# The gate's x made behind the last weight split, and the first pair group's weights prepared one unit earlier

## The chip, the cores and the metric

The kernel runs on one core of a Trainium2 chip. The metric is the time of the device in microseconds (us), lower is better. The kernel before was timed three times: 843.56, 845.28 and 845.81 us, median 845.28 us. Its profiled execution took 846.12 us.

## The reference

Three layers follow one another, all in float32.

```python
# attention: B, H, S, D = 2, 8, 768, 64; a band of 96 local keys and 8 global ones
scores = q @ k.T / sqrt(D) - slope[h] * dist ; masked outside the band
x = softmax(scores) @ v                       # -> x: 1536 tokens x 512
# experts: 4 of them, 512 -> 1024 -> 512, weighted by given probabilities p
for e in range(4):
    out += p[:, e:e+1] * (relu(x @ w1[e]) @ w2[e])
# gate
a = out @ w1 ; b = out @ w2                   # 512 -> 1024
result = (a * b) @ w3 @ w_out                 # 1024 -> 1024 -> 512
```

## The kernel before, in words

Every large matrix product is made with three TensorE matmuls: an operand is split into a high part (a rounding cast) and a low part (what the cast lost), and high x high, low x high and high x low are summed in PSUM. `split` (line 47) does this: ScalarE writes the high part (line 49) and VectorE or GpSimd the low part (line 50). `three` (line 53) issues the three matmuls (lines 55, 56, 57). One matmul is 128x128 by 128x512.

Tokens are cut into three chunks c of 512; `x_hi[c]`, `x_lo[c]` hold the split x of a chunk, `acc[c]` the sum over experts. Weights lie in eight slots (`slots[0]` to `slots[7]`), each a high and a low tile of 128x1024: an expert's up weights in columns 0 to 511, its down weights in columns 512 to 1023. Raw weights come by DMA into tiles `wr`, of which the pool has two, so a load can only start when the split of the load before the previous one has read its tile.

The stages after attention:

- Units. `work` lists units (e, c, f): expert, chunk, block of 128 of the hidden 1024. Unit n issues the up product, a ReLU with its split (lines 541 and 542), and the down product of the unit two back. Experts 0 and 1 take all chunks here, experts 2 and 3 chunk 0 only.
- Pair groups. For experts 3 and 2, chunks 1 and 2 are done together by a scheme with seven products in place of eight (`Pairs`). A group's weights need the splits of raw blocks (`split_w`) and of sums of blocks (`sums_of_w`). Those of group n+1 are made inside group n. Those of group 0 are made in the last units, behind the ReLU of unit len-2 (`split_w`) and of unit len-1 (`sums_of_w`).
- The end of the pair groups ("the join" below). The last down products of expert 2 are issued, chunk 1 (f = 6, 7), then chunk 2 in the order f = 7, 4, 0, 1, 2, 3, 5, 6. As a slot becomes free, it takes weights for the next stage: slots 4, 0, 1, 2, 3, 5, 6, 7 are split in that order from eight raw loads (w3 transposed in slots 4 to 7, w_out in slots 0 to 3). When a chunk's down products are done, VectorE multiplies the four PSUM results by p into temporaries `t` (line 749) and GpSimd adds them to `acc` (line 750). For expert 2, `last_x(c, d)` then makes the split of the finished x: ScalarE casts (line 756), GpSimd subtracts (line 757). It is called for chunks 1 and 2 right behind their addition, and for chunk 0 after the last split.
- w34. TensorE makes w3 @ w_out, eight products of 24 matmuls into four PSUM banks `z`, each of them split into `w34h`, `w34l`. Chunk 2's down results stand in the same four banks, so the first product of w34 needs the first of them read by line 749.
- Gate: chunk 0 first, then chunks 1 and 2 as a pair, with w34 as the last product. It is the first reader of the x of `last_x`.

The order on every engine is the order in which the code issues, since the kernel sets its own schedule and each engine takes its queue in order. SP issues all the DMAs, in order as well.

Of the kernel before, what the change touches and what calls it, by code (L numbers as in the profile page):

```python
# [26 lines left out]
KC, FC = DM // P, F // P  # L27
CW = 512
NCH = N // CW
# [23 lines left out]
def three(nc, out, wh, wl, xh, xl, start, stop):  # L53

    nc.tensor.matmul(out, wh, xh, start=start, stop=False)  # L55
    nc.tensor.matmul(out, wh, xl, start=False, stop=False)  # L56
    nc.tensor.matmul(out, wl, xh, start=False, stop=stop)  # L57
# [24 lines left out]
def expert_shares(nc, g, tmp, room):  # L82

    nt = N // P
    pr = room[:nt, 0 : E * P].rearrange("c (t e) -> c t e", e=E)
    pe = room[:nt, E * P :].rearrange("c (e t) -> c e t", e=E)
    sm = tmp()[:nt, 0:P]
    nc.vector.tensor_reduce(sm, pr, axis=AX.X, op=ALU.add)
    nc.vector.tensor_scalar(sm, sm, 1e-9, None, op0=ALU.add)
    nc.vector.reciprocal(sm, sm)  # L90
    nc.vector.tensor_tensor(
        pe, pr.rearrange("c t e -> c e t"), sm.unsqueeze(1).to_broadcast([nt, E, P]), op=ALU.mult
    )
    nc.sync.dma_start(g.prob_dram.rearrange("e (c t) -> c e t", t=P), pe)


def banded_flag(nc, g, pool, ps, room):


    top, row, ok = room[:, 0:1], room[0:1, 8:16], room[0:1, 16:24]  # L100
    tp = ps.tile([P, CW], F32, name="z")[0:1, 0:P]
    nc.tensor.transpose(tp, top, g.ident)
    nc.vector.tensor_reduce(row[:, 0:1], tp, axis=AX.X, op=ALU.max)
    w0 = g.words[0:1]
    nc.vector.tensor_scalar(ok[:, 0:1], row[:, 0:1], 5.0e8, None, op0=ALU.is_le)
    nc.vector.tensor_scalar(ok[:, 1:2], w0[:, 0:1], 0.0, None, op0=ALU.is_ge)
    nc.vector.tensor_scalar(ok[:, 2:3], w0[:, 0:1], float(GW), None, op0=ALU.is_le)
    nc.vector.tensor_scalar(ok[:, 3:4], w0[:, 1:2], 0.0, None, op0=ALU.is_equal)
    nc.vector.tensor_scalar(ok[:, 4:5], w0[:, 2:3], 1.0, None, op0=ALU.is_ge)
    nc.vector.tensor_scalar(ok[:, 5:6], w0[:, 2:3], float(LW + 1), None, op0=ALU.is_le)  # L110
    nc.vector.tensor_scalar(ok[:, 6:7], w0[:, 3:4], 0.0, None, op0=ALU.is_equal)
    nc.vector.memset(ok[:, 7:8], 1.0)
    nc.vector.tensor_reduce(row[:, 1:2], ok, axis=AX.X, op=ALU.min)
    nc.vector.tensor_copy(g.flag, row[:, 1:2])
# [454 lines left out]
def pair_weights(g, pairs):  # L569

    half = lambda e, gr, c: g.w_moe[e, 2 * gr : 2 * gr + 2][:, :, c * CW : (c + 1) * CW].rearrange("f p c -> p f c")
    groups = [(e, gr) for e in pairs for gr in range(FC // 2)]
    res = [half(*groups[0], 0)]
    for n, (e, gr) in enumerate(groups):
        if n + 1 < len(groups):
            res.append(half(*groups[n + 1], 0))
        if e != pairs[0]:
            res.append(half(e, gr, 1))
    return res + [g.w3t_f32[0]] + [g.wo_f32[j] for j in range(4)] + [g.w3t_f32[j] for j in range(1, 4)]
# [105 lines left out]
def experts_and_gate(tc, g, x_hi, x_lo, slots, experts, first_time):  # L685
# [3 lines left out]
    with ExitStack() as ctx:  # L689
# [18 lines left out]
        def load_slot(s, src):  # L708

            raw = pool.tile([P, F], F32, name="wr")  # L710
            nc.sync.dma_start(raw, src)
            coming.append((s, raw))

        def land(keep=0):
            while len(coming) > keep:
                s, raw = coming.pop(0)
                split(nc, *slots[s], raw)

        work, pending = experts.work, experts.pending
        pieces = list(g.pieces) if first_time else []  # L720

        pairs = list(range(E - 1, EARLY - 1, -1))
# [3 lines left out]
        def down(e, c, f, fs=None, tail=False):  # L726
            fs = fs or list(range(FC))
            hi, lo = slots[f]
            hh, hl = pending.pop((e, c, f))
            if f == fs[0]:  # L730
                state["o"] = [
                    ps_z.tile([P, CW], F32, name="z") if tail else ps_a.tile([P, CW], F32, name=f"o{d}")
                    for d in range(KC)
                ]
            if f == fs[3]:
                state["p"] = xp.tile([P, CW], F32, name="prob")
                nc.sync.dma_start(state["p"], g.prob_dram[e, c * CW : (c + 1) * CW].partition_broadcast(P))
            o = state["o"]
            for d in range(KC):
                ds_ = slice(CW + d * P, CW + (d + 1) * P)  # L740
                three(nc, o[d], hi[:, ds_], lo[:, ds_], hh, hl, f == fs[0], f == fs[-1])
            ring.give((e, c, f))
            if f == fs[-1]:
                for d in range(KC):
                    if e == 0:
                        nc.vector.tensor_tensor(acc[c][:, d], o[d], state["p"], op=ALU.mult)
                        continue
                    t = tmp()
                    nc.vector.tensor_tensor(t, o[d], state["p"], op=ALU.mult)  # L749
                    nc.gpsimd.tensor_tensor(acc[c][:, d], acc[c][:, d], t, op=ALU.add)  # L750
                    if c and e == pairs[-1]:
                        last_x(c, d)

        def last_x(c, d):

            nc.scalar.copy(x_hi[c][:, d], acc[c][:, d])
            nc.gpsimd.tensor_tensor(x_lo[c][:, d], acc[c][:, d], x_hi[c][:, d].bitcast(F32), op=ALU.subtract)  # L757
# [15 lines left out]
        by_pairs = raws = xsums = None  # L773
        first_pair = len(work) - 2 * FC
        for n, w in enumerate(work):
            if n >= done:
                experts.up(w, ps_z.tile([P, CW], F32, name="z"))
                if n >= FC:
                    land()
                elif coming:  # L780
                    s = coming[-1][0] + 1
                    land(len(coming) - 1)
                    if s < FC:
                        load_slot(s, g.w_moe[0, s])
            if n == 4 and first_time:
                expert_shares(nc, g, tmp, room)
            if n == FC and first_time:
                flag_room = tmp()
                nc.vector.tensor_reduce(flag_room[:, 0:1], g.negmax, axis=AX.X, op=ALU.max)
            if n == FC + 2 and first_time:  # L790
                banded_flag(nc, g, pool, ps_z, flag_room)
            if n >= LAG:
                e, c, f = work[n - LAG]
                down(e, c, f)

                if e + 1 < E and (e >= EARLY or c == NCH - 1):
                    load_slot(f, g.w_moe[e + 1, f])
            if n > 4 and n % FC != LAG - 1:
                if ended:
                    nc.sync.dma_start(*ended.pop(0))  # L800
                if begun:
                    piece, dst = begun.pop(0)
                    ended.append((dst, convert_end(nc, cpool, *piece)))
                if fetched:
                    raw, dst = fetched.pop(0)
                    begun.append((convert_start(nc, cpool, raw), dst))
                if pieces:
                    src, dst = pieces.pop(0)
                    raw = cpool.tile([P, 512], mybir.dt.int64, name="raw", bufs=3)
                    nc.sync.dma_start(raw, src)  # L810
                    fetched.append((raw, dst))
            if by_pairs is None and n >= first_pair and not (pieces or fetched or begun or ended):
                late.close()
                tpool = of_experts.enter_context(tc.tile_pool(name=name + "xt", bufs=1))
                by_pairs = Pairs(nc, tpool, tmp, ps_z, experts)
                xsums = by_pairs.sums_of_x()
            elif xsums:
                next(xsums, None)
            if n == len(work) - 4:
                assert not coming  # L820
                raws = Raws(nc, pool, 2, pair_weights(g, pairs))
            if n == len(work) - 2:
                by_pairs.split_w(0, raws.here[0])
            if n == len(work) - 1:
                by_pairs.sums_of_w(0, raws.here[0])
                raws.used()
        assert next(xsums, None) is None
# [6 lines left out]
        for n in range(last + 1):  # L834
            i, gr = divmod(n, FC // 2)
            e = pairs[i]
# [43 lines left out]
        split(nc, *slots[7], raws.here[0])  # L880
        raws.used()
        assert not raws.here
        for d in range(KC):
            last_x(0, d)
        ring.free.remove((xp, "h3"))
        of_experts.close()

# [247 lines left out]
def tile_attention_experts_gate(  # L1135
# [43 lines left out]
    slots += slot_tiles(rest, 4, FC)  # L1179

    experts_and_gate(tc, g, x_hi, x_lo, slots, experts, True)

    banded = nc.values_load(g.flag[0:1, 0:1], min_val=0, max_val=1)
# [69 lines left out]
```

## Time and profile before

| | before |
|---|---|
| runs, median | 845.28 us (843.56 to 845.81) |
| profiled execution, its time | 846.12 us |
| its span (first to last instruction) | 844.3 us |
| TensorE matmul busy | 825.6 us, 98% |
| VectorE / ScalarE / GpSimd busy | 515.8 / 289.1 / 308.6 us |
| mean granted TensorE clock | 0.991 |

The 1.8 us between the profiled time and the span lie outside the instructions. A share of busy time is a mean over all stages, so the places where TensorE is not busy have to be found in time: of the page's 40 slices, the one from 591 to 612 us has a busy share of 6 tenths and a granted clock of 7 tenths, where the others after attention have 9 in both. It holds the end of the pair groups and the beginning of w34.

### The profile page before, as it was taken

How to read it: one execution, taken by the hardware profiler on the slowest of the kernel's cores; microseconds unless marked ns; L12 is line 12 of the kernel's file. 1: busy time of each engine (PE TensorE's matmuls, PEld its weight loads, DVE VectorE, ACT ScalarE, POOL GpSimd, SP SyncE). 2: the span in 40 equal slices, each digit the busy share in tenths (PEclk: the TensorE clock that was granted, in tenths of full speed). 3: DMA queues.
4: the chain of work that ended last, by engine and by line, in shares of the span. 5: the costliest groups of instructions: out<-in, count | busy, mean ns of one | idle time of the engine just before them, and what ended most of it. 6: DMA issues, size and time to landing. Idle time of an engine off the chain costs nothing.

```text
span 844.3 us, 11129 instructions
## 1 busy us (share of the span) xinstructions
PE 825.6 (98%) x4006; PEld 670.5 (79%) x4006; DVE 515.8 (61%) x962; ACT 289.1 (34%) x609; POOL 308.6 (37%) x318
## 2 busy tenths in 40 slices
PE   8999999999999999999999999999699999999996
PEld 4777888888888888888888888888488888888875
DVE  7998355557755557778557664673343733887840
ACT  6997321223321213333324321332242332333210
POOL 3687013535356554642154252314250002433300
PEclk9999999999999999999999999999799999999998
DMA  7762243557453458643101111121433220201011
GB/s 221 224 196 75 77 122 104 163 166 241 156 163 112 158 153 235 217 147 100 38 25 52 38 46 42 50 71 35 145 101 99 75 75 26 99 26 51 1 54 51
DMA packets 38710, 89.23 MB, mean 106 GB/s; under 512 B 3896, under 2 KB 10344, under 8 KB 38644
## 3 DMA queue, kind: packets, MB, share of 16 engines
q1 hardware_dynamic: 38644, 88.41, 33.5%
q8 instruction: 34, 0.56, 0.3%
q14 instruction: 32, 0.26, 0.1%
HBM read 74.74 MB, written 13.66 MB: 105 GB/s over the span
## 4 chain that ended last, share of the span: by engine, by line
PE 40%; issue 7%; POOL 2%; DVE 2%; ACT 1%; DMA 1%; ACTq 0%; POOLq 0%; DVEq 0%
PE z L55 9%; PE z L57 9%; PE z L56 9%; PE o L57 4%; PE o L55 4%; PE o L56 4%; POOL acc L750 1%; DMA wr<-wo_d 1%; ACT sh L49 1%; POOL sl L50 1%; DVE sl L50 1%; POOL xl L757 0%; DVE t L649 0%; DMA wr<-w3t_d 0%; DVE t L642 0%
## 5 line engine op out<-in xcount | busy, mean ns | idle before, releaser
L57 PE MATMUL z<-xh,sl 128*128 128x512 f32 x428 | 166.6, 389 | 0.0
L55 PE MATMUL z<-xh,sh 128*128 128x512 f32 x428 | 166.5, 389 | 0.0
L56 PE MATMUL z<-xl,sh 128*128 128x512 f32 x428 | 166.5, 389 | 0.0
L50 POOL TENSOR_TENSOR sl<-wr,sh 128x256 fp32r<-128x256 f32 (+1 forms) x44 | 40.9, 945 | 155.8 <-ACT sh L49 155.5
L498 POOL TENSOR_TENSOR cr<-cr,cb 128x512 f32<-128x512 f32 x40 | 51.6, 1290 | 125.2 <-issue 118.7
L57 PEld LDWEIGHTS z<-xh,sl 128*128 128x128 f32 x428 | 80.3, 188 | 17.1 <-DVE sl L50 0.2
L56 PEld LDWEIGHTS z<-xl,sh 128*128 128x128 f32 x428 | 80.3, 188 | 16.7
L55 PEld LDWEIGHTS z<-xh,sh 128*128 128x128 f32 x428 | 80.3, 188 | 16.6
L50 DVE TENSOR_TENSOR sl<-wr,sh 128x1024 fp32r<-128x1024 f32 (+1 forms) x57 | 67.8, 1198 | 41.8 <-ACT sh L49 41.1
L49 ACT CAST sh<-wr 128x1024 fp32r<-128x1024 f32 (+2 forms) x101 | 75.2, 767 | 11.9 <-DMA wr<-wo_d 8.1
L750 POOL TENSOR_TENSOR acc<-acc,t 128x512 f32<-128x512 f32 x36 | 47.5, 1350 | 84.1 <-DVE t L749 84.1
L483 POOL TENSOR_SCALAR ca<-ca 128x512 f32<-128x512 f32 x40 | 61.5, 1538 | 36.9 <-DMA raw<-in_w_out_dram 36.9
L55 PE MATMUL z<-sh,sh 128*128 128x512 f32 x128 | 51.1, 400 | 7.8 <-DVE t L749 7.8
L649 DVE TENSOR_TENSOR t<-t,z 128x512 f32<-128x512 f32 x56 | 37.5, 680 | 30.4 <-PE z L57 30.2
L57 PE MATMUL z<-sh,sl 128*128 128x512 f32 x128 | 50.9, 397 | 0.0
L56 PE MATMUL z<-sl,sh 128*128 128x512 f32 x128 | 50.8, 397 | 0.0
L269 ACT ACTIVATE pt<-t,negmax 128x256 f32<-128x256 f32 (+1 forms) x96 | 45.9, 480 | 9.0 <-DVE negmax L262 7.7
L308 POOL TENSOR_TENSOR pt<-pt,r 128x256 f32<-128x256 f32 (+1 forms) x72 | 40.8, 595 | 15.2 <-DVE r L237 12.6
L262 DVE CUSTOM_DVE_ANT_0 t<-sp,bias 128x256 f32<-128x256 f32 (+1 forms) x96 | 34.6, 394 | 1.8 <-ACT bias L224 0.4
L55 PEld LDWEIGHTS z<-sh,sh 128*128 128x128 f32 x128 | 24.7, 193 | 13.4 <-issue 8.2
L50 POOL TENSOR_TENSOR sl<-t,sh 128x256 fp32r<-128x256 f32 (+1 forms) x24 | 23.0, 972 | 31.2 <-ACT sh L49 31.0
L55 PE MATMUL o<-h0h,sh 128*128 128x512 f32 x84 | 32.8, 390 | 0.0
(254 smaller groups left out, 1751.9 us busy)
## 6 DMA issues: line engine op xcount, KB each, us to landing
wr<-in_w_moe_dram SPq DMA_DIRECT2D x44, 512.0 KB, 4.3
raw<-in_w3t_dram SPq DMA_DIRECT2D x16, 512.0 KB, 4.3
raw<-in_w_ab_dram SPq DMA_DIRECT2D x16, 512.0 KB, 4.6
wr<-wab_d SPq DMA_DIRECT2D x16, 512.0 KB, 3.3
raw<-in_w_out_dram SPq DMA_DIRECT2D x8, 512.0 KB, 5.1
w3t_d<-cr SPq DMA_DIRECT2D x16, 256.0 KB, 2.4
wab_d<-cr SPq DMA_DIRECT2D x16, 256.0 KB, 2.5
wr<-w3t_d SPq DMA_DIRECT2D x8, 512.0 KB, 3.4
```

Source lines behind the costliest of these rows:

```text
L49: nc.scalar.copy(hi, src)
L50: (lo_engine or nc.vector).tensor_tensor(lo, src, hi.bitcast(F32), op=ALU.subtract)
L55: nc.tensor.matmul(out, wh, xh, start=start, stop=False)
L56: nc.tensor.matmul(out, wh, xl, start=False, stop=False)
L57: nc.tensor.matmul(out, wl, xh, start=False, stop=stop)
L262: nc.vector.tensor_tensor_reduce(out=t[:, 0:w], in0=sp[hh % 2][:, hh // 2, 0:w], in1=bb, scale=-SCALE, scalar=3.0e38, op0=ALU.add, op1=ALU ...
L269: nc.scalar.activation(pt[:, hh, 0:w], t[:, 0:w], AF.Exp, bias=g.negmax[:, u * H + h : u * H + h + 1], scale=-1.0, accum_out=sums[:, h : h ...
L308: nc.gpsimd.tensor_tensor(pt[:, hh, 0:w], pt[:, hh, 0:w], r[:, hh : hh + 1].to_broadcast([P, w]), op=ALU.mult)
L483: nc.gpsimd.tensor_scalar(a, a, 2.0**-15, None, op0=ALU.max)
L498: nc.gpsimd.tensor_tensor(rest, rest, top.bitcast(F32), op=ALU.add)
L649: add = lambda o, a, b: nc.vector.tensor_tensor(o, a, b, op=ALU.add)
L750: nc.gpsimd.tensor_tensor(acc[c][:, d], acc[c][:, d], t, op=ALU.add)
```

## The change

Two edits. In the first, `last_x` is no longer called behind the additions of chunks 1 and 2; all twelve calls (three chunks of four) stand behind the split of slot 7. In the second, `split_w` and `sums_of_w` of the first pair group are issued one unit earlier, behind units len-3 and len-2; the load of the next raw tile, which `raws.used()` issues, moves with the sums.

```diff
@@ down
                     nc.gpsimd.tensor_tensor(acc[c][:, d], acc[c][:, d], t, op=ALU.add)
-                    if c and e == pairs[-1]:
-                        last_x(c, d)
@@ units
             if n == len(work) - 4:
                 assert not coming
                 raws = Raws(nc, pool, 2, pair_weights(g, pairs))
+            if n == len(work) - 3:
+                by_pairs.split_w(0, raws.here[0])
             if n == len(work) - 2:
-                by_pairs.split_w(0, raws.here[0])
-            if n == len(work) - 1:
                 by_pairs.sums_of_w(0, raws.here[0])
                 raws.used()
@@ after the last split
-        for d in range(KC):
-            last_x(0, d)
+        for c in range(NCH):
+            for d in range(KC):
+                last_x(c, d)
```

The first place is ScalarE's queue at the join. In the names, sh_1556, sh_1558, sh_1560, sh_1562 are the high tiles of slots 4, 5, 6, 7; sh_77, sh_79, sh_81, sh_83 those of slots 0 to 3; xh_71, xh_72, xh_73 the high x of chunks 0, 1, 2. Before:

```order
L756 CAST xh_72<-acc_1577 128x512 x4
L49 CAST sh_1556<-wr 128x1024
L49 CAST sh_77<-wr 128x1024
L49 CAST sh_79<-wr 128x1024
L49 CAST sh_81<-wr 128x1024
L49 CAST sh_83<-wr 128x1024
L49 CAST sh_1558<-wr 128x1024
L756 CAST xh_73<-acc_1578 128x512 x4
L49 CAST sh_1560<-wr 128x1024
L49 CAST sh_1562<-wr 128x1024
L756 CAST xh_71<-acc_1576 128x512 x4
```

And now:

```order
L49 CAST sh_1556<-wr 128x1024
L49 CAST sh_77<-wr 128x1024
L49 CAST sh_79<-wr 128x1024
L49 CAST sh_81<-wr 128x1024
L49 CAST sh_83<-wr 128x1024
L49 CAST sh_1558<-wr 128x1024
L49 CAST sh_1560<-wr 128x1024
L49 CAST sh_1562<-wr 128x1024
L754 CAST xh_71<-acc_1576 128x512 x4
L754 CAST xh_72<-acc_1577 128x512 x4
L754 CAST xh_73<-acc_1578 128x512 x4
L49 CAST w34h<-z 128x512 x2
```

The four casts of chunk 1 no longer stand ahead of slot 4's split, nor those of chunk 2 between slots 5 and 6. On GpSimd the twelve subtractions (line 757, now 755) follow the eight additions in one run, where they stood one behind each addition. VectorE's order at the join is unchanged.

The second place is ScalarE's queue in the last units, where the names h0 to h3 are the hidden tiles of the units and sh_77 to sh_83 slots 0 to 3. The difference:

```order
 L541 ACTIVATE h1h<-z 128x512
-L541 ACTIVATE h2h<-z 128x512
-L49 CAST sh_77<-wr 128x512
-L49 CAST sh_79<-wr 128x256
-L541 ACTIVATE h3h<-z 128x512
+L49 CAST sh_77<-wr 128x512
+L49 CAST sh_79<-wr 128x256
+L541 ACTIVATE h2h<-z 128x512
 L49 CAST sh_79<-t 128x256
 L49 CAST sh_81<-t 128x512
 L49 CAST sh_83<-t 128x256
+L541 ACTIVATE h3h<-z 128x512
```

The casts of the raw blocks now stand ahead of the ReLU of the last but one unit, and those of the sums ahead of the last unit's. On VectorE the four instructions that make the sums (line 642) move ahead of the low part of h3 in the same way.

## Rows read from the trace of the kernel before

**Rows 1.** Page, part 1: busy us, share of the span, instructions.

```profile
PE 825.6 (98%) x4006; PEld 670.5 (79%) x4006; DVE 515.8 (61%) x962; ACT 289.1 (34%) x609; POOL 308.6 (37%) x318
```

**Rows 2.** Waits of TensorE: line, for whom; us in total, times, longest.

```profile
PE z L55 <- DVE t L749: 7.8, 1, 7.8
...
PE z L57 <- POOL sl L50: 0.2, 1, 0.2
```

**Rows 3.** Timeline of TensorE, join: start, us, what, [idle before <-releaser].

```profile
583.45 0.39 PE L57 MATMUL z<-xh,sl 128*128 128x512 f32 x1
...
594.56 0.39 PE L55 MATMUL z<-h0h,sh 128*128 128x512 f32 x1
...
597.05 0.39 PE L57 MATMUL z<-h0h,sl 128*128 128x512 f32 x1
605.24 0.76 PE L55 MATMUL z<-sh,sh 128*128 128x512 f32 x1 [7.80 <-DVE t L749]
...
611.19 0.40 PE L57 MATMUL z<-sh,sl 128*128 128x512 f32 x1
```

**Rows 4.** Windows: stretch, us, busy PE, PEld, DVE, ACT, POOL, PEclk, DMA, GB/s.

```profile
600.00:601.00 1.00, 0.00 (x0) 0.00 (x0) 0.64 (x1) 0.00 (x0) 0.00 (x0) 0.88 0.83 262
601.00:602.00 1.00, 0.00 (x0) 0.00 (x0) 0.00 (x0) 0.00 (x0) 0.00 (x0) 0.50 0.90 246
```

**Rows 5.** Timeline of ScalarE at the join.

```profile
575.78 0.62 ACT L756 CAST xh<-acc 128x512 fp32r<-128x512 f32 x1 [3.46 <-POOL acc L750]
...
585.61 0.62 ACT L756 CAST xh<-acc 128x512 fp32r<-128x512 f32 x1 [2.65 <-POOL acc L750]
586.13 2.00 ACT L49 CAST sh<-wr 128x1024 fp32r<-128x1024 f32 x2
...
596.44 1.05 ACT L49 CAST sh<-wr 128x1024 fp32r<-128x1024 f32 x1 [3.21 <-DMA wr<-wo_d]
...
602.19 1.04 ACT L49 CAST sh<-wr 128x1024 fp32r<-128x1024 f32 x1 [2.80 <-DMA wr<-w3t_d]
```

**Rows 6.** Timeline of VectorE at the join.

```profile
604.41 2.48 DVE L749 TENSOR_TENSOR t<-z,prob 128x512 f32<-128x512 f32 x4
```

**Rows 7.** Timeline of SP's DMA issues at the join.

```profile
568.22 21.94 SPq L561 DMA_DIRECT2D wr<-wo_d  x3
...
588.71 1.45 SPq L561 DMA_DIRECT2D wr<-wo_d  x2
590.21 0.42 SPq L737 DMA_DIRECT2D prob<-prob_d  x1
...
598.77 0.32 SPq L561 DMA_DIRECT2D wr<-w3t_d  x1
```

**Rows 8.** Raw loads, line 561: landing times in 555 to 557, and 566 to 610.

```profile
DMA to landing us min/median/max: 3.3/3.3/3.3
...
DMA to landing us min/median/max: 3.2/3.4/6.5
```

**Rows 9.** Timeline of GpSimd at the join.

```profile
605.17 1.27 POOL L750 TENSOR_TENSOR acc<-acc,t 128x512 f32<-128x512 f32 x1 [17.57 <-DVE t L749]
...
619.37 7.01 POOL L757 TENSOR_TENSOR xl<-acc,xh 128x512 fp32r<-128x512 f32 x4 [1.12 <-ACT xh L756]
```

**Rows 10.** Timeline of TensorE at the first pair group.

```profile
429.21 0.39 PE L56 MATMUL z<-t2l,sh 128*128 128x512 f32 x1
429.77 0.50 PE L57 MATMUL z<-t2h,sl 128*128 128x512 f32 x1 [0.17 <-POOL sl L50]
430.11 0.40 PE L55 MATMUL z<-t2h,sh 128*128 128x512 f32 x1
```

**Rows 11.** Timelines there: GpSimd, ScalarE, SP.

```profile
427.34 3.07 POOL L50 TENSOR_TENSOR sl<-t,sh 128x256 fp32r<-128x256 f32 x3 [4.45 <-ACT sh L49]
...
419.73 0.60 ACT L541 ACTIVATE h2h<-z 128x512 fp32r<-128x512 f32 x1 [4.84 <-PE z L57]
...
395.77 10.89 SPq L561 DMA_DIRECT2D wr<-in_w_moe_dram  x2
```

## The prediction

> **What bounds the kernel now.** The page's first part comes first: TensorE is busy for 98% of the span [rows 1]. A faster TensorE is not on offer, so what can be won is the time in which it stands or runs at its lower clock. The second view is the list of TensorE's waits: one entry is far above the others, 7.8 us, once, for VectorE's line 749 [rows 2]. The third is TensorE's timeline at that place [rows 3]. The last down matmul starts at 597.05, the first matmul of w34 at 605.24. In the group of twelve before, starts lie (597.05 - 594.56) / 11 = 0.226 us apart, so 8.19 - 0.23 = 7.96 us are lost. Then the clock: from 605.24 to 611.19 fourteen matmuls start, which at 0.226 would take 3.17 us and took 5.95, so 2.78 us more are lost. The windows say why [rows 4]: the granted clock, still 1.00 before, is 0.88 in 600 to 601 and 0.50 after, so it fell to its lower level at about 600.76, in the middle of the standstill. The join costs 10.7 us in all.
>
> Why VectorE was late is read backwards. Line 749 for chunk 2 starts at 604.41 [rows 6], though the first of the four sums it reads was complete soon after 594.56 + 3 x 0.23 = 595.24. It stands in VectorE's queue behind the low part of slot 5. That waited for ScalarE's cast of slot 5 at 602.19, and that for a load (w3t_d) [rows 5]. The load was issued at 598.77 [rows 7], right when the split of slot 2 had read its tile, and slot 2's cast at 596.44 again waited for a load, issued at 588.71 + 1.45 - 0.32 = 589.84, when slot 0's split had read its tile. So it is a chain with two tiles: cast, low part, load, cast. Its beginning is at 586.13: ScalarE cast slots 4 and 0 there, back to back, since up to 585.61 it was taken up by the four casts of chunk 1's x, each behind a GpSimd addition (575.78 the first, 585.61 the last) [rows 5]. TensorE had released slot 0 long before: the group of f = 0 ends with the matmul at 583.45, thus at 583.84 [rows 3], and slot 4's group ended 2.72 us (12 x 0.226) earlier, at 581.12.
>
> **The change, edit 1: the join.** The chain now starts when TensorE lets it. Two steps recur in it. From a cast's start to the issue of the load that reuses its tile: 598.77 - 596.44 = 2.33 us [rows 5, 7] (cast, low part, SP). From slot 5's cast to TensorE's restart: 605.24 - 602.19 = 3.05 us (cast, low part, line 749, bank released) [rows 3, 5]. Now slot 4 is cast at 581.15 and slot 0 at 583.90; its load went out at 568.22 [rows 7] and is there. The load that slot 2 needs is issued at 583.90 + 2.33 = 586.23. It lands after D2, and slot 2's cast starts. 2.33 later the load for slot 5 is issued, and lands after D1; 3.05 after that TensorE restarts:
>
> 586.23 + D2 + 2.33 + D1 + 3.05 = 591.61 + D1 + D2.
>
> For the landing times the trace gives 3.3 for a load alone with a p load behind it, and 3.2 to 6.5, median 3.4, at the join [rows 8]. The 6.5 is the very load of slot 2 (589.84 to 596.44, 6.60 with ScalarE's start): it went out 1.1 us behind another raw load and 0.4 us ahead of a p load [rows 7]. The p load stays behind it, and the raw load before it is now issued 2.7 us earlier, not 1.1. I take D2 = 4.2, nearer to the lone load, bounds 3.3 and 6.6. D1 was 602.19 - 598.77 = 3.42; now a load for slot 3 may still be under way, so I take 3.6, bounds 3.3 and 3.8. The restart is then 591.61 + 7.8 = 599.4, with bounds 598.2 and 602.0; it could not be before about 597.8, since slot 5's own group of down matmuls ends only at 594.56 + 0.16 and the 3.05 follow. Gain of the wait: 605.24 - 599.4 = 5.84 us.
>
> With a restart at 599.4 TensorE has stood for some 2.1 us. In the trace the clock was at its upper level until 600.76 [rows 4], later than that, so I count all of the 2.78 us as won.
>
> The Trainium skill has a rule on this (TensorE: Matmul & The Clock Gate, Part 1: The HAM clock gate): the clock halves only after TensorE has been idle for a stretch, and comes back after a stretch of sustained work, whose position against the kernel's work varies from run to run. The trace agrees with both halves of it, once each. By that rule a restart at 599.4 keeps the clock for certain, and one after 600.8 may keep or lose it, whereas by the row alone it loses it.
>
> **What the moved work may cost.** The twelve x casts (0.62 us each [rows 5], 7.4 us at most) now stand on ScalarE between slot 7's split and the cast of w34's first product, which is queued behind them. The last four wait for GpSimd's additions, which begin behind line 749, at about 599.3, and take 1.3 each [rows 9], so they end near 605.3 and the first w34 cast comes at some 606. TensorE ends that product at 599.4 + 24 x 0.226 + 0.16 = 605.0, and wants its bank back for the fifth product, 4 x 24 x 0.226 = 21.7 us after the restart, at 621. That leaves 14 us of cover: cost 0, and 1 us for each beyond it. The next slots' splits are queued behind as well, but belong to products after the fourth. GpSimd's twelve subtractions run on from 605.3 at 1.75 each (7.01 for four [rows 9]) to 626. The gate, their first reader, begins behind eight products of 5.4 us, at about 643, and reads chunk 0 first, which is done first. Cost 0. VectorE's low parts of slots 6 and 7 follow line 749 at about 601.2; TensorE needs slot 6 at 599.4 + 2 x 5.43 = 610.3. Cost 0 as well. As for a gain from these, none: nothing waits for x earlier.
>
> **Edit 2: the first pair group.** TensorE waits once for the low part of the sums: 429.77 - 429.21 = 0.56 in place of 0.23, and 430.11 - 429.77 = 0.34 in place of 0.23 [rows 10], so 0.44 us. GpSimd made these low parts at 427.34 to 430.41 [rows 11]. One unit (24 x 0.226 = 5.4 us) earlier they end at 425.0, and nothing of TensorE's comes so late: gain 0.44, and no more, because no other wait stands there. What is now ahead of the ReLU h2h at 419.73 are two casts, in a gap of 4.84 us in which ScalarE waited for TensorE [rows 11]; the raw tile they read was asked for at 395.77, 19 us before. Cost 0, at worst that of a load that lands late, which even 6.6 us would not make it. The load behind `raws.used()` goes out earlier, and with it no queue is held up: SP issues it in order and has nothing ahead of it.
>
> **Sum.** 5.84 + 2.78 + 0.44 = 9.06 us. The profiled execution goes from 846.12 to 837.1. It lies 0.84 above the median of the runs, 845.28; from the median the same gain gives 836.2, my prediction.
>
> **Rivals.**
>
> 1. The loads stay slow, and the clock falls. D2 = 6.6, D1 = 3.8: restart at 602.0, behind 600.76, and the fourteen slow matmuls remain. Gain 3.2 + 0.44 = 3.7: 841.6. For it: the 6.5 us landing stood next to this p load. Against: less is under way beside it now.
> 2. The clock falls in the short standstill too. Gain 5.84 + 0.44 = 6.3: 839.0. Against it are the rows of the windows, for it only that the fall may come at another point of the standstill in another run.
> 3. The change doesn't do what it says: line 749 is late for a reason other than the x casts, for instance as the tiles of `wr` turn over no faster than before. Then only edit 2 is left: 844.8, no change. For it: line 749 waited for a chain of loads, with ScalarE idle for 3.21 and 2.80 us between casts [rows 5]. Against: the chain is tied to its beginning, and that moves, slot 4's cast from 586.13 to 581.15 and the load for slot 2 from 589.84 to 586.23.
> 4. Slower. The loads are bunched at the join: slots 4, 0, 1 are released at TensorE's pace of 2.72 us, so the raw loads of slots 1, 2 and 3 and the p load queue up at the DMA engines while down matmuls run. TensorE restarts later than before when D1 + D2 exceeds 605.24 - 591.61 = 13.6; at 8.3 each the restart is at 608.2, 3.0 us later, with the clock down: 847.8. Against: two tiles allow no more than two raw loads at a time, and with two and p under way the longest took 6.6.
>
> **How the numbers follow.** The forecast has 0.70, with its own range 834.6 (restart at 597.8: 7.44 + 2.78 + 0.44 = 10.7) to 838.5; rival 1 has 0.14, rival 2 0.07, rival 3 0.06, rival 4 0.03. A range from 834.0 to 841.7 holds the forecast, rival 2 and about the middle of rival 1. A measurement of this kernel can tell about 0.3%, 2.5 us, from no change. Faster than 842.7: 0.70 + 0.14 + 0.07 = 0.91; same: 0.06; slower: 0.03.
>
> **What would show it.** Right: in the changed kernel's ScalarE timeline slot 4's cast follows TensorE's release within a few tenths, about 5 us earlier than before; line 749 for chunk 2 starts near 598.6; TensorE's wait for it is about 2 us; the granted clock stays at 1.00 through the join; the wait for GpSimd's low parts at the first pair group is gone, and no new entry of over 0.5 us stands in the list of waits. Wrong: a restart after 602, a landing of over 6 us on the load of slot 2, a wait of w34's fifth product for a bank, or a wait of the gate for GpSimd.

## The result and the profile after

The changed kernel takes 835.19 us (median of 4 runs, 835.08 to 837.08) against 844.82 us for the kernel before beside it. The ratio is 0.989, with an interval of 0.987 to 0.991: faster, by 9.6 us at the medians. The forecast was 836.2 us, with a range of 834.0 to 841.7. The profiled execution went from 846.12 to 835.12, its span from 844.3 to 833.3.

TensorE's list of waits answers [rows 2]. The 7.8 us for line 749 have become

```profile
PE z L55 <- DVE t L749: 0.8, 1, 0.8
```

and the wait for GpSimd's low part at the first pair group is no longer in the list. One entry is new, 0.6 us for a load of attention's keys (line 251); it stands at 6.0 us, at the start of the kernel and far ahead of both edits, and the profile with edit 1 alone does not have it. TensorE's timeline, at the first pair group and at the join, answers [rows 10] and [rows 3]:

```profile
429.00 0.39 PE L56 MATMUL z<-t2l,sh 128*128 128x512 f32 x1
429.23 0.39 PE L57 MATMUL z<-t2h,sl 128*128 128x512 f32 x1
429.45 0.39 PE L55 MATMUL z<-t2h,sh 128*128 128x512 f32 x1
...
596.39 0.39 PE L57 MATMUL z<-h0h,sl 128*128 128x512 f32 x1
597.56 0.47 PE L55 MATMUL z<-sh,sh 128*128 128x512 f32 x1 [0.79 <-DVE t L749]
597.87 0.40 PE L56 MATMUL z<-sl,sh 128*128 128x512 f32 x1
```

The first three start 0.23 us apart, where 0.56 lay between the first two before. At the join 1.17 us lie between starts, so 1.17 - 0.23 = 0.94 us are lost, and 0.31 - 0.23 = 0.08 at the next step. The windows that answer [rows 4] have the clock at its upper level:

```profile
597.00:598.00 1.00, 0.44 (x2) 0.42 (x3) 1.00 (x3) 0.46 (x1) 0.44 (x1) 1.00 0.10 20
...
600.00:601.00 1.00, 1.00 (x6) 0.84 (x5) 1.00 (x1) 0.68 (x1) 1.00 (x2) 1.00 0.00 0
```

The chain of casts and loads is read from two timelines, ScalarE's, which answers [rows 5],

```profile
580.31 1.05 ACT L49 CAST sh<-wr 128x1024 fp32r<-128x1024 f32 x1 [8.65 <-PE z L56]
582.99 1.05 ACT L49 CAST sh<-wr 128x1024 fp32r<-128x1024 f32 x1 [1.62 <-PE z L56]
...
588.77 1.05 ACT L49 CAST sh<-wr 128x1024 fp32r<-128x1024 f32 x1 [1.71 <-DMA wr<-wo_d]
...
594.51 1.05 ACT L49 CAST sh<-wr 128x1024 fp32r<-128x1024 f32 x1 [1.50 <-DMA wr<-w3t_d]
...
601.27 6.35 ACT L754 CAST xh<-acc 128x512 fp32r<-128x512 f32 x12
607.53 0.58 ACT L49 CAST w34h<-z 128x512 fp32r<-128x512 f32 x1
```

and SP's, which answers [rows 7]:

```profile
567.54 18.10 SPq L561 DMA_DIRECT2D wr<-wo_d  x3
585.70 0.42 SPq L737 DMA_DIRECT2D prob<-prob_d  x1
...
591.11 6.06 SPq L561 DMA_DIRECT2D wr<-w3t_d  x3
```

Slots 4 and 0 are now cast as soon as TensorE releases them ("<-PE"), 2.7 us apart, and no x cast stands before them. The load for slot 2 goes out at 567.54 + 18.10 - 0.32 = 585.32; slot 2's cast follows 3.45 us later, slot 5's 3.40 us behind its load at 591.11, and TensorE restarts 3.05 us after that.

Where the 11.0 us of the span went: the last matmul starts at 826.63 instead of 837.11, 10.48 us earlier. Of these 0.44 are the first pair group's; about 0.2 were there before it (its matmul at 429.21 against 429.00), from earlier in the kernel and not from the change; the rest, 9.8, is the join and w34. The last 0.5 us of the span lie behind the issue of the last store.

### The profile page after: what moved, and what is told of

Its sections match the earlier page's. It is cut to its first block, busy times and chain, and to the rows that moved or that the text cites. A ratio compares the mean times of both kernels' runs of the same rounds, so it can differ in the third digit from the quotient of the medians.

```text
span 833.3 us, 11131 instructions
## 1 busy us (share of the span) xinstructions
PE 821.4 (99%) x4006; PEld 668.4 (80%) x4006; DVE 518.4 (62%) x962; ACT 288.4 (35%) x609; POOL 310.1 (37%) x318
## 4 chain that ended last, share of the span: by engine, by line
PE 89%; POOL 3%; ACT 3%; DVE 2%; issue 1%; DMA 0%; SPq 0%; POOLq 0%; ACTq 0%; DVEq 0%
PE z L55 18%; PE z L57 18%; PE z L56 18%; PE o L57 11%; PE o L55 11%; PE o L56 11%; POOL pt L308 2%; ACT pt L269 2%; POOL sl L50 1%; DVE t L262 1%; ACT ptT L294 0%; DMA words<-in_n_local_dram 0%; PE sp L55 0%; PE sp L56 0%; PE sp L57 0%
## 5 line engine op out<-in xcount | busy, mean ns | idle before, releaser
L50 DVE TENSOR_TENSOR sl<-wr,sh 128x1024 fp32r<-128x1024 f32 (+1 forms) x57 | 70.7, 1245 | 23.1 <-ACT sh L49 22.4
L750 POOL TENSOR_TENSOR acc<-acc,t 128x512 f32<-128x512 f32 x36 | 49.3, 1404 | 84.8 <-DVE t L749 84.8
L57 PE MATMUL o<-h0h,sl 128*128 128x512 f32 x84 | 32.7, 389 | 0.0
```

The source lines that it names most:

```text
L50: (lo_engine or nc.vector).tensor_tensor(lo, src, hi.bitcast(F32), op=ALU.subtract)
```

## Experiments

In each, the time of before was taken on the same chip, beside the run.

### Each edit by itself

Edit 1 alone is the changed kernel with edit 2 taken back:

```diff
-            if n == len(work) - 3:
+            if n == len(work) - 2:
                 by_pairs.split_w(0, raws.here[0])
-            if n == len(work) - 2:
+            if n == len(work) - 1:
                 by_pairs.sums_of_w(0, raws.here[0])
                 raws.used()
```

> Edit 1 without edit 2: all x casts behind the last split, the first pair group's weights where they were before. If the two edits are independent, the join is as in the changed kernel (TensorE's wait for line 749 near 0.8 us, clock at its upper level throughout) and the wait of 0.2 us for GpSimd's low part at the first pair group is back, with 0.44 us between starts lost there: 835.6 us against 835.2 for both edits. Rival: part of the gain at the join comes from edit 2 (an earlier load), and then the join here loses more than 1 us.

Measured: 835.81 us, ratio to before 0.990 (0.988 to 0.992). Its TensorE timeline has the old step at the first pair group, to the hundredth,

```profile
428.99 0.39 PE L56 MATMUL z<-t2l,sh 128*128 128x512 f32 x1
429.55 0.50 PE L57 MATMUL z<-t2h,sl 128*128 128x512 f32 x1 [0.17 <-POOL sl L50]
```

and at the join 1.10 us between starts (596.85 to 597.95). So edit 1 gives the gain at the join by itself.

Edit 2 alone is the kernel before with edit 2 made in it.

> Edit 2 without edit 1. If edit 2 is worth what its wait was, 0.44 us, this is 844.4 us against 844.8 before, which the timing can't tell from no change; the trace shows no wait for GpSimd's low part at the first pair group, and at the join the 7.8 us wait and fourteen matmuls at half clock as before. Rival: an edit that only shifts the join against the clock or the loads makes it a few us better or worse.

Measured: 843.62 us against 844.79, ratio 0.999 (0.998 to 1.000), which can't be told from no change. In the trace the step at the first pair group is gone, and the standstill at the join is there, somewhat shorter than in the profile of before:

```profile
596.38 0.39 PE L57 MATMUL z<-h0h,sl 128*128 128x512 f32 x1
603.49 0.77 PE L55 MATMUL z<-sh,sh 128*128 128x512 f32 x1 [6.72 <-DVE t L749]
```

The two edits add up and don't touch each other.

### Chunk 1's casts and chunk 2's casts apart

Edit 1 moves two things. The first kernel leaves chunk 2's x behind its addition and moves chunk 1's:

```diff
                     nc.gpsimd.tensor_tensor(acc[c][:, d], acc[c][:, d], t, op=ALU.add)
+                    if c == 2 and e == pairs[-1]:
+                        last_x(c, d)
...
-        for c in range(NCH):
+        for c in (0, 1):
```

> As the changed kernel, but chunk 2's four x casts stand where they stood before, between the splits of slots 5 and 6; chunk 1's stay moved. Theory (chunk 1's casts held the head of ScalarE's queue and with it the chain of raw loads): TensorE restarts as in the changed kernel, about 1 us lost, at full clock. But slot 6's cast now comes some 12.4 us behind the first line 749 (as before: 616.78 behind 604.41), near 609.1, and its low part is done near 611.5, where TensorE wants it at 608.5 to 609: a new wait of 2 to 3 us at w34's third product, and 837.5 us. Rival (the two wr tiles set the pace, whatever stands on ScalarE): restart as before, 844.5. Rival (chunk 2's casts are what matters): restart late as well.

Measured: 840.06 us against 844.79, ratio 0.994 (0.992 to 0.996). ScalarE does what was expected; the first and last x cast of chunk 2, then slots 6 and 7:

```profile
599.48 0.62 ACT L756 CAST xh<-acc 128x512 fp32r<-128x512 f32 x1 [3.33 <-POOL acc L750]
...
609.28 0.62 ACT L756 CAST xh<-acc 128x512 fp32r<-128x512 f32 x1 [2.65 <-POOL acc L750]
609.81 1.99 ACT L49 CAST sh<-wr 128x1024 fp32r<-128x1024 f32 x2
```

TensorE's waits:

```profile
PE z L55 <- ACT sh L49: 1.6, 1, 1.6
...
PE z L55 <- DVE t L749: 1.1, 1, 1.1
...
PE z L57 <- DVE sl L50: 0.8, 1, 0.8
```

The wait at the join is gone as with both chunks, and a new one stands at w34's third product: first for slot 6's high part, then for its low part; together 2.9 us are lost between starts. What was not expected is in the windows behind it:

```profile
612.00:613.00 1.00, 0.61 (x3) 0.53 (x4) 1.00 (x2) 1.00 (x3) 0.61 (x1) 1.00 0.00 0
613.00:614.00 1.00, 1.00 (x5) 0.81 (x4) 0.47 (x1) 1.00 (x3) 1.00 (x1) 0.70 0.61 193
614.00:615.00 1.00, 1.00 (x4) 0.81 (x3) 0.00 (x0) 1.00 (x3) 1.00 (x2) 0.50 0.90 340
```

The clock fell at about 613.4 (a mean of 0.70 in 613 to 614), 1 us after TensorE was back at work at 612.39, and eight matmuls took 0.43 us each. They lost 8 x 0.20 = 1.6 of the 2.5 us between the 837.5 expected and 840.06.

The second kernel is its mirror image (c == 1 stays, 0 and 2 move).

> As the changed kernel, but chunk 1's four x casts stand where they stood before, ahead of slot 4's split; chunk 2's stay moved. Theory: ScalarE starts slot 4 at about 585.5 again, TensorE waits 7.8 us for line 749 and runs fourteen matmuls at half clock, 844.3 us: edit 2's 0.4 us better than before and nothing else. Rival (chunk 2's casts matter): several us better.

Measured: 842.67 us against 844.79, ratio 0.999 (0.997 to 1.000), which can't be told from no change; 844.3 had been expected. The standstill is back, and its cause stands at the head of ScalarE's queue, slots 4 and 0 being cast only at 585.46:

```profile
585.46 2.00 ACT L49 CAST sh<-wr 128x1024 fp32r<-128x1024 f32 x2
```

TensorE restarts at 603.03, with 6.3 us of waiting, less than the 7.8 of before, since the load for slot 2 took 5.11 us here (issued at 589.17, cast at 594.28) and 6.60 there. So chunk 1's casts hold the chain of loads, and the reading that the two raw tiles would set the pace whatever stands on ScalarE is refuted by the pair of kernels. But chunk 2's casts matter too: with them in place about half of the gain is taken back at slot 6. Before, that second wait was hidden behind the first one: TensorE came to slot 6 so late, and at half clock, that only 0.1 us of it was seen (0.33 us between the starts at 619.39 and 619.72).

### The clock alone

The kernel before, with matmuls that nobody needs in the standstill:

```diff
             last_x(0, d)
+        fill = ps_a.tile([P, CW], F32, name="o0")
+        for _ in range(26):
+            nc.tensor.matmul(fill, x_hi[1][:, 0, 0:P], x_hi[1][:, 0], start=True, stop=True)
```

> The kernel before, with 26 matmuls whose result nobody reads issued between the last down product and w34's first, so that TensorE works through most of its 7.8 us wait (26 x 0.226 = 5.9 us, to about 603.2). It prices the clock alone. Theory: the restart stays at 605.2, since it waits for line 749, but the clock doesn't fall and the fourteen matmuls run at 0.226: 2.8 us less than before, 842.0 us. Rival (the clock term was counted twice, w34 is held by slot 6 anyway): the third product waits for slot 6's low part at about 619, as its split is no earlier, so that most of the 2.8 us come back as a wait there and the time is 844 to 845 us.

Measured: 845.22 us against 844.07, ratio 1.001 (1.000 to 1.002). The rival was right:

```profile
PE z L55 <- ACT sh L49: 1.5, 1, 1.5
...
PE z L57 <- DVE sl L50: 0.8, 1, 0.8
PE z L55 <- DVE t L749: 0.4, 1, 0.4
```

w34 starts at full clock and then waits for slot 6, as above, and the clock falls there (a mean of 0.85 in 617 to 618, 0.50 after). The 2.8 us of half clock in the kernel before were thus not to be had by keeping the clock up: slot 6 was due at the same moment. They could be won only together with slot 6, which edit 1 brings by taking chunk 2's casts away as well.

### The x work put later still

```diff
+            if j == 3:
+                for c in range(NCH):
+                    for d in range(KC):
+                        last_x(c, d)
```

in w34's loop, in place of the call behind the last split.

> The changed kernel with all twelve last_x calls later still, behind the split of w34's fourth product (near 619 us instead of 601). Theory: the place of the x work within w34 costs nothing, since the gate reads x only near 641: 835.2 us as the changed kernel, no new wait of TensorE. GpSimd's subtractions then end near 640, chunk 0's first, near 627. Rival (GpSimd's subtractions beside the splits of slots 6 and 7 slow VectorE and so TensorE): up to 0.5 us faster; rival (the gate wants x earlier): slower by the wait.

Measured: 835.56 us, ratio to before 0.989 (0.988 to 0.991), the same as the changed kernel. GpSimd's twelve subtractions:

```profile
623.58 18.54 POOL L755 TENSOR_TENSOR xl<-acc,xh 128x512 fp32r<-128x512 f32 x12 [17.21 <-ACT xh L754]
```

They end at 642 and nobody waits for them. So between 601 and 623 us it makes no difference that the timing can tell where the x work stands.

### The multiplication ahead of slot 5's split

What is left at the join is line 749 behind slot 5's low part on VectorE.

```diff
-            for s in (f,) if c == 2 and f != 7 else ():
+            for s in {7: (), 5: (), 6: (5, 6)}.get(f, (f,)) if c == 2 else ():
                 split(nc, *slots[s], raws.here[0])
```

> The changed kernel with the split of slot 5 issued behind the last down product, so that on VectorE the four multiplications of line 749 come ahead of slot 5's low part; ScalarE's order stays. Theory (what is left at the join, 0.94 + 0.08 us, is line 749 queued behind slot 5's low part): the first multiplication starts near 594.8, TensorE goes on without a wait, 834.2 us. Rival: slot 5's low part is then too late for w34's second product (needed near 602, expected by 599.5), or the multiplications wait for GpSimd's additions to free t, and the time stays at 835.2.

Measured: 834.06 us against 844.07, ratio 0.988 (0.986 to 0.989). VectorE's timeline, line 749 first and waiting for TensorE alone, the low parts of slots 5 and 6 behind it:

```profile
596.38 2.80 DVE L749 TENSOR_TENSOR t<-z,prob 128x512 f32<-128x512 f32 x4 [0.55 <-PE z L57]
599.10 3.97 DVE L50 TENSOR_TENSOR sl<-wr,sh 128x1024 fp32r<-128x1024 f32 x2
```

TensorE goes through the join with 0.22 us between starts (598.00 to 598.22). It was run again beside the changed kernel:

> The changed kernel again, unaltered, on the chip of the kernels beside it: 835.2 us, raw load for slot 2 landing in 3.4 us and TensorE's wait at the join 0.8 us, as in its first profile. It is the measure for the next one.

> The kernel with line 749 ahead of slot 5's low part again, beside the changed kernel: 834.1 us, 1.0 us below it, with no wait of TensorE at the join.

Measured: 835.94 us (835.17 to 836.8) and 834.87 us (834.01 to 835.8), ratios to before 0.990 (0.989 to 0.992) and 0.990 (0.988 to 0.991). The difference is 1.07 us at these medians and 1.13 at the first ones, which is what the trace has at the join (0.94 + 0.08), though the intervals overlap. The four profiled executions differ in one thing more, the clock near the kernel's start. In the first profile of the changed kernel, and then in that of its second run:

```profile
10.00:20.00 10.00, 8.20 (x64) 4.78 (x64) 9.32 (x54) 9.91 (x44) 5.62 (x16) 1.00 0.72 230
```

```profile
10.00:20.00 10.00, 8.43 (x55) 4.98 (x54) 7.78 (x46) 8.37 (x38) 5.11 (x15) 0.83 0.63 200
```

Of the kernel with the multiplication first, the first profile has 0.83 there and the second 1.00. Like with like, though not all on one chip, the two with 1.00 are 835.12 and 834.01, the two with 0.83 are 836.80 and 835.63: 1.1 and 1.2 us apart. So this version beats the changed kernel by about 1 us.

### A longer standstill at the join

The prediction expected TensorE to stand for 2.1 us with the clock up. The changed kernel stands for less, so this step was tried by itself, with slot 5's low part written twice:

```diff
                 split(nc, *slots[s], raws.here[0])
+                for _ in range(1 if s == 5 else 0):
+                    nc.vector.tensor_tensor(slots[5][1], raws.here[0], slots[5][0].bitcast(F32), op=ALU.subtract)
```

> The changed kernel with the low part of slot 5 written twice (the same subtraction again, 1.15 us on VectorE) ahead of line 749, so that TensorE stands for 0.94 + 1.15 = 2.1 us at the join, the standstill that the prediction expected. Theory (as predicted: the clock stays up, since it fell later than that before): 835.2 + 1.2 = 836.4 us, granted clock 1.00 through the join. Rival (what the fillers and the variant with chunk 1 alone showed at w34's third product, where the clock fell after waits of 1.7 and 0.9 us in one stretch of 3.5): it falls here too in this execution or another, up to 2.8 us more, 837 to 839 us.

Measured: 839.06 us against 835.94 for the changed kernel beside it. TensorE's timeline and the windows:

```profile
596.32 0.39 PE L57 MATMUL z<-h0h,sl 128*128 128x512 f32 x1
599.05 0.47 PE L55 MATMUL z<-sh,sh 128*128 128x512 f32 x1 [2.34 <-DVE t L749]
```

```profile
599.00:600.00 1.00, 0.95 (x4) 0.86 (x5) 1.00 (x2) 0.00 (x0) 0.96 (x1) 1.00 0.54 123
600.00:601.00 1.00, 1.00 (x4) 0.79 (x3) 1.00 (x3) 0.00 (x0) 1.00 (x2) 0.60 0.92 340
601.00:602.00 1.00, 1.00 (x3) 0.72 (x3) 1.00 (x1) 0.04 (x1) 1.00 (x2) 0.50 0.16 61
```

With 2.73 - 0.23 = 2.50 us lost at the join (2.1 had been aimed at), the clock fell at about 600.2, when TensorE had been back at work for over 1 us. So the theory that a restart ahead of 600.76 keeps the clock falls with this execution. One of the other three, 838.48 us at a mean clock of 0.997 (the profiled one has 0.995), may have kept it; no trace shows that. With the low part written three times:

> The same with the low part written three times: a standstill of 0.94 + 2.3 = 3.2 us. If the clock falls only after standstills like that of before, it stays up: 837.5 us. If it falls after shorter ones too, fourteen or fewer matmuls run at half clock: 838.5 to 840.3 us, and the granted clock at 0.50 behind the join.

Measured: 840.55 us, with 3.84 - 0.23 = 3.61 us lost and the clock at half behind the join:

```profile
596.74 0.39 PE L57 MATMUL z<-h0h,sl 128*128 128x512 f32 x1
600.58 0.77 PE L55 MATMUL z<-sh,sh 128*128 128x512 f32 x1 [3.45 <-DVE t L749]
```

```profile
599.00:600.00 1.00, 0.00 (x0) 0.00 (x0) 1.00 (x2) 0.00 (x0) 0.00 (x0) 0.59 0.00 0
```

So a standstill of 0.9 us kept the clock here, and one of 2.5 us lost it. Where in the standstill the clock falls is not fixed. Here it fell at 599.18 (0.59 in 599 to 600), 2.4 us after the start of the last down matmul; in the kernel before 3.7 us after it (600.76 - 597.05); with edit 2 alone 5.7 us after it (602.12 - 596.38), by the row

```profile
602.00:603.00 1.00, 0.00 (x0) 0.00 (x0) 1.00 (x2) 0.00 (x0) 0.00 (x0) 0.56 0.27 107
```

## Why the prediction was right, and where it was not

**The cause and the chain: right.** Chunk 1's x casts held the head of ScalarE's queue and with it two loads in a row; the two kernels with one chunk moved, and edit 1 alone, show it. Rivals 1, 3 and 4 did not happen. The formula 591.61 + D1 + D2 holds step by step: 582.99 + 2.33 + 3.45 + 2.34 + 3.40 + 3.05 = 597.56, where TensorE restarts.

**The term that was mis-sized: D2.** It was taken as 4.2 us and measured 3.45 (3.43 to 3.57 in the eight other profiles in which slots 4 and 0 are cast early). Before, it was 6.60, and 5.1 to 5.6 in the three other kernels that keep the old order of the casts. The bounds were right, and the rows agree with the reason: the raw load ahead of it was issued 2.67 us earlier (582.65) instead of 1.13 and had landed by 586.01, when its slot was cast, so for most of its way slot 2's load had only the p load beside it. No run changed that gap alone, so the reason is read from these rows and not tested, and why a gap of 1.13 us gave 5.1 us in one profile and 6.6 in another stays open. I should have gone to the lone load's end. With D1 3.40 for 3.6, and slot 0 cast 0.25 us earlier against TensorE than reckoned, this makes the 1.2 us between the standstill forecast, 2.1, and the one measured, 0.94.

**The clock: the term right, its reason wrong.** The clock stayed up, and 2.78 us of half clock went. But the step "with a restart at 599.4 the clock is kept" was drawn from one fall at 600.76 and does not hold: with a standstill of 2.5 us the clock fell, after the restart, and in other profiles it fell 2.4 to 5.7 us after the last down matmul. Had D2 been 4.2, the standstill would have been 2.1 us. No run has that, but rival 2, at 839.0, might well have come true: the kernel with one more subtraction took 839.06. It had been given 0.07. The rule of the Trainium skill as the prediction put it (TensorE: Matmul & The Clock Gate, Part 1: The HAM clock gate) would have kept the clock for certain at such a restart; the measurement decides against that reading. That the clock stayed up was thus partly luck: the first error, a wait reckoned too long, may have spared the forecast the second.

**What the term for the clock hid.** The sum counted the 2.78 us beside the wait, as if the two were one stall's parts. The kernel with fillers shows that they were not: without chunk 2's casts gone, slot 6 takes them back. The prediction had the low parts of slots 6 and 7 begin at about 601.2 in its reckoning of the moved work (slot 6's began at 599.13 and ended at 601.20), but did not say that the clock term rests on it.

**The moved work: cost nothing, as forecast.** The x casts run at 601.27 to 607.62, the first w34 cast follows at 607.53 (forecast: some 606), and the list of waits has none for the fifth product's bank. GpSimd's subtractions end at 621.6 (forecast: 626).

**Edit 2: 0.44 us, right to the hundredth,** below what the timing can tell.

**The sum.** Forecast 9.06 us; the profiled executions differ by 11.0, the medians by 9.6. The surplus in the profiles is the 1.2 us of the standstill, 0.2 before the first pair group and 0.5 at the last store. The two profiles also make the gain look large: the 6.60 us that slot 2's load took in the profile of before are 1 us or more above what it took in the three other kernels with the old order, and TensorE waited 6.7 us with edit 2 alone, not 7.8. So some 1 us of the 11.0 lies, by this estimate, in that one execution. The upper end of the forecast's own range, 838.5, is not worked out; the sum with a restart at 602.0 and the clock kept gives 845.28 - 6.46 = 838.8.

## What to carry to other kernels

When an engine that takes its queue in order feeds a chain of loads through few tiles, look at what stands at the head of its queue when the chain could begin: four short casts that each waited for GpSimd cost about 7 us on TensorE, two engines away (842.67 us with chunk 1's casts alone in the old place, 835.2 with none). Move such work behind the last step of the chain if its reader is far off, and check the next wait behind the first: taking away one stall alone may only show the next. Count a clock term as won only where no wait of a few microseconds is left, and for a transfer's landing take the row that has the same company, not a mean between rows.

## What the runs showed of the hardware that was not expected

The granted clock fell although TensorE was at work again: at 600.2 with a restart at 599.05, and at 613.4 with a restart at 612.39, after 2.50 us lost at one place and 2.9 us at two places close together. After 0.94 us it did not.

VectorE's splits and GpSimd's additions slow each other when they meet. In the changed kernel the low parts of slots 6 and 7 and the last two additions of chunk 2 run side by side:

```profile
599.13 2.07 DVE L50 TENSOR_TENSOR sl<-wr,sh 128x1024 fp32r<-128x1024 f32 x1
601.40 2.03 DVE L50 TENSOR_TENSOR sl<-wr,sh 128x1024 fp32r<-128x1024 f32 x1 [0.20 <-ACT sh L49]
```

```profile
598.81 1.31 POOL L750 TENSOR_TENSOR acc<-acc,t 128x512 f32<-128x512 f32 x1
600.07 2.29 POOL L750 TENSOR_TENSOR acc<-acc,t 128x512 f32<-128x512 f32 x1
602.32 2.27 POOL L750 TENSOR_TENSOR acc<-acc,t 128x512 f32<-128x512 f32 x1
```

The splits took 2.07 and 2.03 us against 1.23 alone, the two additions beside them 2.29 and 2.27 against 1.27 [rows 9]; the addition at 598.81, begun before the first of these splits, took 1.31. The Trainium skill (SBUF — State Buffer, SBUF: two separate sides) has VectorE operations with two inputs in SBUF and GpSimd operations take turns on a shared pair of ports, each for a whole instruction. The rows agree with that: additions and splits end in turn, at 600.12, 601.20, 602.36, 603.43 and 604.59, 1.07 to 1.16 us apart, about what each takes alone. Here the meeting cost TensorE nothing, since slot 6 was ready some 7 us before its product.
